# Last stage of an attention + expert + feed-forward kernel: slot outputs copied ahead of decoding, folding in three rounds, last 256 tokens with activations stationary, some low parts on VectorE, a new order

## The chip, the cores and the metric

The kernel runs on one core of a Trainium2 chip. The metric is the device time of one execution in microseconds; the kernel before has a median of 518.03 us over 3 runs (517.16 to 518.10). The profiled execution is one of its own.

## The reference, cut to what matters

```python
attn = softmax(mask(q @ k.T / 8)) @ v            # 4 batches, 12 heads, 448 tokens, 64 wide; causal
x = attn as (1792 tokens, 768)
logits = x @ phi                                  # 32 slots = 8 experts x 4
slot_input = softmax(logits over tokens).T @ x
slot_out = per expert: relu(slot_input @ w1[e]) @ w2[e]        # (32, 768)
y = softmax(logits over slots) @ slot_out          # (1792, 768)
h = y @ w_in                                       # w_in (768, 2048)
g = h * cos(h)
return g @ w_out                                   # w_out (2048, 768)
```

`w_in` and `w_out` come as float64 (two 32-bit words an element) and are turned into fp32 on the chip. All of it is computed at about fp32 precision.

## The kernel before, in words

The program has three stages. The first (to about 180 us) is the attention, with the slot logits and the slot inputs of each batch. The second (to about 236 us) streams 48 pieces of `w1` and `w2`, 1 MB each, through SBUF and ends with `slot_out`, transposed into `soT` (768 rows in six chunks of 128, 32 slots). It waits for the memory; `keep_warm` puts dummy matmuls between its pieces. The third, which the change is about, runs from there to the end.

The third stage never forms y. It folds `slot_out` into `w_in`: WS = slot_out @ w_in is only 32 x 2048, and h = softmax(logits) @ WS. WS and the softmax weights `CT` are kept in pieces of fp32r (a rounded fp32 that TensorE multiplies at full rate) stacked on 96 partitions, so that one matmul gives h at nearly fp32 precision. The hidden width 2048 is cut into 16 chunks `fc` of 128, the tokens into blocks of 512, 512, 512 and 256. A step is one chunk on one block, and `seq` (from SEQ, line 30) lists the 64 steps; the last 16 (s = 48 to 63) are the 256 tokens of block 3. The parts of a step, by their letters in the planner:

- H (`t_h`, L872): one matmul, h into one of two PSUM banks (6 and 7).
- Y, R, S, G (`t_y` L876 on ACT, `t_r` L879 on DVE, `t_s` L882 on ACT, `t_g` L885 on DVE): g = h cos(h) by range reduction and the sine table.
- K (`t_k`, L888, ACT): the high part of g in fp32r. L (`t_l`, L891, always POOL before): the low part, g minus its high part, from SBUF to SBUF.
- B (`back`, L898 to L900): for each of six 128-column groups m of `w_out`, three matmuls into bank m: high weights by high g, low weights by high g, high weights by low g. The weights are the stationary operand, the tokens are the moving one (512 columns, or 256 in block 3). The first step has its own order (`back0`, L908).
- F (`finish`, L915 to L921): bank m is added to or copied to SBUF at the end of a run of chunks, and after chunk 15 it goes out by a DMA on SP's queue. The output is held transposed, (768, 1792).

Each chunk needs two weight items of 768 KB: item 2c is `w_in`, item 2c+1 is `w_out`. Its decoding is a (`dec_a`, L706, ACT) and l, h, s (`dec_l`, `dec_h`, `dec_s`, L709, L713, L717, DVE, SBUF to SBUF). `w_out` is then split: u (`up_part`, L728, ACT) the high part in fp32r, v (`lo_part`, L741, DVE or POOL) the low part. `w_in` is folded for one or two chunks at a time (GRP, line 31): wm (`w_mm`, L839) multiplies six 128-row pieces by `soT`. A stationary `soT` chunk has 32 columns, so four such matmuls sit side by side, in four column groups of the array (r = ch % 4); w4 (L847, ACT) copies, wr (`w_rep`, L850, TensorE) adds the four groups, ws and wd (L854 ACT, L858 DVE) make WS.

A planner at the end of the file sets the order: it simulates the engines with a cost for each task (T, A, D, P for TensorE, ACT, DVE, POOL) and takes, whenever an engine is free, the ready task with the lowest key, its due time in steps. `port` keeps tasks of DVE and POOL apart that both work from SBUF to SBUF, with a tolerance (.35 before, L1034). The plan is written out as program order; each engine then works its list in order. `free` (L993) and the tasks `so` and `s,1` say when the second stage lets go of each engine.

Between the stages, in the last round of the second (L812 to L825, for piece 48), the order before is: `decode(1)`, i.e. item 1 on ACT and DVE; the copy of the last slot outputs `so` (L818, ACT); one `keep_warm`; two transposes (L823); the copy into `soT` (L824, DVE). `wm` of the first chunk needs that copy and item 0, which was decoded at piece 44.

## Time and profile before

| | |
|---|---|
| median of 3 runs | 518.03 us (517.16 to 518.10) |
| time of the profiled execution | 517.3 us |
| its span, first to last instruction | 515.5 us |
| TensorE (PE) busy | 488.3 us, 95% |
| VectorE (DVE), ScalarE (ACT), GpSimd (POOL) busy | 348.4, 313.5, 187.6 us |

Times in a profile are microseconds from the span's start unless marked ns. PE is TensorE's matmuls, PEld its weight loads, SP the engine that issues the DMAs. A matmul's end is modelled, so that two matmuls seem to overlap; the distance from one start to the next is what counts. L900 is line 900 of the kernel. In a timeline, the brackets give the idle time of the engine before the instruction and what ended it.

### The profile page before, as it was taken

Reading aid. Unit: us, or ns where it says so; the run is one execution under the profiler, and the core shown is the slowest. Engines: PE = TensorE matmul, PEld = TensorE weight load, DVE = VectorE, ACT = ScalarE, POOL = GpSimd, SP = SyncE. Lnnn points to the kernel's source line nnn. Section 1 sums busy time; section 2 is a strip of 40 time slices with the busy share of each in tenths; the row PEclk is TensorE's granted clock in tenths of the full one; section 3 lists DMA queues with packets and bytes.
Section 4 is the critical chain, followed back from the end, with each engine's and each line's share of the span. In section 5 each row is a group of like instructions: output and inputs, shape, how many; then the busy total and the mean of one; then the engine's idle time right before and its main releaser. Section 6 shows DMA issues by size and latency. Waiting matters only on the chain.

```text
span 515.5 us, 11275 instructions
## 1 busy us (share of the span) xinstructions
PE 488.3 (95%) x4308; PEld 357.3 (69%) x4308; DVE 348.4 (68%) x899; ACT 313.5 (61%) x745; POOL 187.6 (36%) x269
## 2 busy tenths in 40 slices
PE   8999999999999888877899999999999999999997
PEld 4766676776776342245667777888878778888996
DVE  4788888888884540025988899797989886355331
ACT  3999999989984201004867764747377555543552
POOL 1665556566540000001425252434442456322331
PEclk9999999999999999997999999999999999999999
DMA  5388788779757999999151533241353011113101
GB/s 198 99 292 296 279 291 292 282 269 337 266 209 261 402 422 419 420 419 359 65 184 61 191 118 123 67 173 65 123 191 116 1 62 73 51 67 116 63 1 62
DMA packets 24245, 100.37 MB, mean 195 GB/s; under 512 B 2816, under 2 KB 6912, under 8 KB 18048
## 3 DMA queue, kind: packets, MB, share of 16 engines
q1 hardware_dynamic: 24192, 99.66, 52.9%
q8 instruction: 34, 0.56, 0.4%
q14 instruction: 19, 0.16, 0.1%
HBM read 94.14 MB, written 5.51 MB: 193 GB/s over the span
## 4 chain that ended last, share of the span: by engine, by line
PE 59%; DVE 17%; ACT 10%; DMA 9%; POOL 2%; issue 2%; ACTq 0%; SPq 0%; POOLq 0%
PE bank L900 8%; PE bank L898 8%; PE bank L899 8%; PE bank L327 7%; PE bank L416 6%; DMA zraw<-in_w_out_dram 5%; PE bank L372 5%; PE bank L797 4%; DMA zraw<-in_w_in_dram 3%; PE bank L812 3%; DVE zscr L879 2%; DVE zscr L885 2%; POOL p L365 2%; ACT zraw L706 2%; ACT zscr L882 2%
## 5 line engine op out<-in xcount | busy, mean ns | idle before, releaser
L898 PE MATMUL bank<-zg,zhl 128*128 128x512 f32 (+1 forms) x378 | 139.7, 370 | 0.4 <-ACT zhl L728 0.4
L899 PE MATMUL bank<-zg,zhl 128*128 128x512 f32 (+1 forms) x378 | 137.5, 364 | 0.9 <-DVE zhl L741 0.9
L900 PE MATMUL bank<-zg,zhl 128*128 128x512 f32 (+1 forms) x378 | 137.2, 363 | 0.9 <-POOL zg L891 0.9
L891 POOL TENSOR_TENSOR zg<-zscr,zg 128x512 fp32r<-128x512 f32 (+1 forms) x64 | 82.7, 1298 | 139.2 <-ACT zg L888 125.4
L365 POOL TENSOR_SCALAR p<-p,pst 128x448 f32<-128x448 f32 (+3 forms) x161 | 79.0, 505 | 56.5 <-DVE pst L356 53.3
L345 ACT ACTIVATE p<-p,pst 128x448 f32<-128x448 f32 (+3 forms) x168 | 87.6, 523 | 13.2 <-DVE pst L343 11.3
L898 PEld LDWEIGHTS bank<-zg,zhl 128*128 128x128 f32 x378 | 71.4, 189 | 13.7 <-issue 1.2
L899 PEld LDWEIGHTS bank<-zg,zhl 128*128 128x128 f32 x378 | 71.5, 189 | 12.4 <-DVE zhl L741 1.4
L900 PEld LDWEIGHTS bank<-zg,zhl 128*128 128x128 f32 x378 | 71.4, 189 | 12.6 <-POOL zg L891 1.3
L882 ACT ACTIVATE zscr<-zscr,b_h 128x512 f32<-128x512 f32 (+1 forms) x64 | 42.0, 669 | 31.0 <-DVE zscr L879 30.8
L879 DVE SCALAR_TENSOR_TENSOR zscr<-zscr,bank 128x512 f32<-128x512 int32 (+1 forms) x64 | 38.8, 618 | 32.5 <-ACT zscr L876 32.2
L343 DVE CUSTOM_DVE_ANT_0 p<-bank,cs 128x448 f32<-128x448 f32 (+1 forms) x96 | 50.9, 548 | 6.4 <-PE bank L327 6.3
L327 PE MATMUL bank<-qk 64*128 64x320 f32 (+2 forms) x288 | 54.1, 472 | 0.0
L888 ACT ACTIVATE zg<-zscr 128x512 fp32r<-128x512 f32 (+1 forms) x64 | 36.3, 576 | 26.0 <-DVE zscr L885 25.8
L885 DVE TENSOR_TENSOR zscr<-bank,zscr 128x512 f32<-128x512 f32 (+1 forms) x64 | 39.2, 621 | 18.5 <-ACT zscr L882 18.4
L876 ACT ACTIVATE zscr<-bank,b_q 128x512 int32<-128x512 f32 (+1 forms) x64 | 39.4, 629 | 19.9 <-PE bank L872 19.8
L741 POOL TENSOR_TENSOR zhl<-uacc,zhl 128x768 fp32r<-128x768 f32 (+1 forms) x7 | 10.6, 1532 | 101.0 <-DMA zraw<-in_w_out_dram 85.9
L706 ACT ACTIVATE zraw<-zraw 128x768 f32<-128x768 f32 x32 | 29.2, 911 | 24.4 <-DMA zraw<-in_w_in_dram 13.1
L212 DVE COPY pts<-bank 128x512 f32<-128x512 f32 x48 | 32.8, 685 | 7.4 <-PE bank L372 6.9
L372 PE MATMUL bank<-cs,p 64*128 64x64 f32 (+1 forms) x768 | 35.3, 227 | 1.5 <-POOL p L365 1.4
L372 PEld LDWEIGHTS bank<-cs,p 64*128 64x128 f32 (+1 forms) x768 | 28.4, 133 | 11.1 <-POOL p L365 5.9
L345 ACT ACTIVATION_READ_ACCUMULATOR p<-p,pst 128x1 f32 x168 | 31.6, 188 | 0.0
(154 smaller groups left out, 695.3 us busy)
## 6 DMA issues: line engine op xcount, KB each, us to landing
w<-in_w_dram SPq DMA_DIRECT2D x48, 1024.0 KB, 8.5
zraw<-in_w_in_dram SPq DMA_DIRECT2D x16, 768.0 KB, 4.4
zraw<-in_w_out_dram SPq DMA_DIRECT2D x16, 768.0 KB, 4.3
qk<-in_qk_dram SPq DMA_DIRECT2D x24, 480.0 KB, 4.0
xk<-in_v_dram SPq DMA_DIRECT2D x12, 256.0 KB, 4.1
out_dram<-zps SPq DMA_DIRECT2D x8, 256.0 KB, 2.0
xts<-in_v_dram SPq DMA_DIRECT2D x12, 128.0 KB, 4.3
lt<-in_v_dram SPq DMA_DIRECT2D x12, 128.0 KB, 4.2
```

Of the source, the lines that this page charges most:

```text
L327: PE.matmul(sreg(j, c), lhsT=Q(p)[h, q0:q0 + 128], rhs=K(p)[h, 0:ln], start=True, stop=True)
L343: DVE.tensor_tensor_reduce(out=dst, in0=sb, in1=m, scale=-0.125, scalar=3.0e38, op0=ALU.add, op1=ALU.min, accum_out=st_[:, col:col + 1])
L345: return pr(f"exp{j}{c}")(lambda: ACT.activation(dst, dst, AF.Exp, bias=st_[:, col:col + 1], scale=-1.0, accum_out=st_[:, 8 + col:9 + col]))
L365: POOL.tensor_scalar(dst, dst, st_[:, 24 + col:25 + col], 0.0, op0=ALU.mult, op1=ALU.add)
L372: PE.transpose(out, src, by)
L879: DVE.scalar_tensor_tensor(y_(s), y_(s).bitcast(I32), -2.0 * math.pi, hb[:, 0:n_(s)], op0=ALU.mult, op1=ALU.add)
L882: ACT.activation(y_(s), y_(s), AF.Sin, bias=b_h, scale=1.0)
L885: DVE.tensor_tensor(y_(s), hb[:, 0:n_(s)], y_(s), ALU.mult)
L891: eng.tensor_tensor(g_(s)[1], y_(s), g_(s)[0].bitcast(F32), ALU.subtract)
L898: PE.matmul(o, lhsT=wh, rhs=gh, start=first, stop=False)
L899: PE.matmul(o, lhsT=wl, rhs=gh, start=False, stop=False)
L900: PE.matmul(o, lhsT=wh, rhs=gl, start=False, stop=last)
```

## The change

- **Between the stages.** `decode(1)` is taken apart: the copy `so` now comes first on ACT, then two `keep_warm` and `dec_a(1)`, the transposes, the copy into `soT` on DVE, two more `keep_warm`, and only then l, h, s of item 1 on DVE.
- **Folding.** For a pair of chunks, `w_mm` deals its twelve matmuls to the four column groups in three rounds of four, where they went in four rounds (four, two, four, two).
- **Last tokens.** In block 3, `back3` makes the 128 tokens of a half block the stationary operand and streams the weights: six triples of matmuls become four, of 512, 512, 256 and 256 columns, in three tasks (U3). `finish3` copies and sends the four banks in three DMAs of 256 KB, and these 256 tokens leave untransposed, so that the output tensor is one flat array with two parts. For chunks 12 to 15 the low parts are laid out so that each streamed segment is contiguous (`w_cols`).
- **Low parts.** L of the 17 steps in LE runs on DVE. Three v tasks have their engine set (VE).
- **Order.** The planner's costs, its start times, LA, the tolerance of `port` (.02) and many keys (KEYS) are new.

```diff
--- before.py
+++ after.py
@@ -30,9 +30,33 @@
 SEQ = ((0, 0, 2), (1, 0, 3), (2, 0, 4), (0, 2, 6), (1, 3, 8), (2, 4, 10), (0, 6, 13), (1, 8, 16), (2, 10, 16), (0, 13, 16), (3, 0, 16))
 GRP = ((0,), (1,), (2, 3), (4, 5), (6, 7), (8, 9), (10, 11), (12, 13), (14, 15))
 SAFE = 0.0
-LA = .4
+LA = 0.3
 KD = 0.0
 LD = False
+KEYS = {
+    ('B', 10, 0): 1, ('B', 10, 2): 1.5, ('B', 12, 2): 7, ('B', 12, 3): 8.75, ('B', 13, 0): 1, ('B', 13, 2): 7.25,
...
+    ('wr', 6): -6.75, ('wr', 8): -2.75, ('ws', 2): -3.5}
+VE = {11: 'P', 3: 'P', 6: 'D'}
+LE = {10: 'D', 11: 'D', 13: 'D', 15: 'D', 16: 'D', 2: 'D', 21: 'D', 26: 'D', 28: 'D', 30: 'D', 31: 'D', 32: 'D', 34: 'D', 43: 'D', 47: 'D', 7: 'D', 9: 'D'}
 KW = 3
@@ -667,7 +691,7 @@
         if c < 12:
             return [(ar[f"hl{c}"], 768 * u, 0, 6)]
         t = [ar[f"hl{3 * (c - 12) + i}"] for i in range(3)]
-        return [(t[0], 1536, 0, 4), (t[1], 1536, 4, 2)] if u == 0 else [(t[1], 1792, 0, 2), (t[2], 1536, 2, 4)]
+        return [(t[0], 1536, 0, 4), (t[1], 1536, 4, 2)] if u == 0 else [(t[2], 1536, 0, 4), (t[1], 1792, 4, 2)]
 
     def w_blk(c, u, m):
         for t, o, m0, nm in w_cols(c, u):
@@ -813,31 +837,41 @@
                                       start=(kc == 0), stop=(kc == 7))
                     if 42 <= npc[0] < 48:
                         keep_warm(3)
-                if npc[0] == 48:
-                    decode(1)
                 ACT.activation(so, sb[:, 0:256], AF.Copy)
                 tb = bank[6]
                 if npc[0] == 48:
-                    keep_warm(1)
+                    keep_warm(2)
+                    dec_a(1)
                 for c in range(2):
                     PE.transpose(tb[:, 128 * c:128 * c + 128], so[:, 128 * c:128 * c + 128], ident)
                 DVE.tensor_copy(soT[:, 2 * n:2 * n + 2, 16 * g:16 * g + 16].rearrange("p c (j t) -> p c j t", j=4),
                                 tb[:, 0:256].rearrange("p (c j t) -> p c j t", c=2, j=4)[:, :, :, 0:SPE])
+                if npc[0] == 48:
+                    keep_warm(2)
+                    dec_l(1)
+                    dec_h(1)
+                    dec_s(1)
 
     CT = ex["CT"]
     arena("WS", "scr", "g0", "g1", "ps", *[f"hl{i}" for i in range(12)], "ps2", "px")
     WS, scr = ar["WS"], ar["scr"]
+    oT = out[0:DM * TOK[3]].rearrange("(d t) -> d t", d=DM)
 
     def w4(q):
         n = len(GRP[q])
         return cs[:, 128 + 256 * (q % 2):128 + 256 * (q % 2) + 128 * n]
 
     def w_mm(q, wb):
-        for k_, n in enumerate(GRP[q]):
-            for ch in range(6):
-                r = ch % 4
-                PE.matmul(wb[32 * r:32 * r + 32, 128 * k_:128 * k_ + 128], lhsT=soT[:, ch, :],
-                          rhs=fwi(n)[:, 128 * ch:128 * ch + 128], start=(ch < 4), stop=(ch + 4 >= 6))
+
+        ts = [(0, 0, 0), (0, 1, 1), (0, 2, 2), (0, 3, 3), (0, 4, 0), (0, 5, 1)]
+        if len(GRP[q]) == 2:
+            ts += [(1, 0, 2), (1, 1, 3), (1, 2, 2), (1, 3, 3), (1, 4, 0), (1, 5, 1)]
+        seen = set()
+        for x, (k_, ch, r) in enumerate(ts):
+            PE.matmul(wb[32 * r:32 * r + 32, 128 * k_:128 * k_ + 128], lhsT=soT[:, ch, :],
+                      rhs=fwi(GRP[q][k_])[:, 128 * ch:128 * ch + 128], start=(k_, r) not in seen,
+                      stop=not any(y[0] == k_ and y[2] == r for y in ts[x + 1:]))
+            seen.add((k_, r))
 
     def wcols(q, wb):
         n = 128 * len(GRP[q])
@@ -907,6 +941,37 @@
             fc = seq[0][1]
             PE.matmul(bank[m][:, 0:n_(0)], lhsT=w_blk(fc, int(k_ == 1), m), rhs=gl if k_ == 2 else gh, start=k_ == 0,
                       stop=k_ == 2 and seq[0][3])
+
+    U3 = (((0, 0, 512, 0),), ((1, 0, 512, 2),), ((0, 512, 768, 1), (1, 512, 768, 3)))
+
+    def w_seg(fc, u, a, b):
+        for t, o, m0, nm in w_cols(fc, u):
+            if 128 * m0 <= a and b <= 128 * (m0 + nm):
+                return t[:, o + a - 128 * m0:o + b - 128 * m0]
+
+    def back3(s, k):
+
+        blk, fc, first, last = seq[s]
+        gh, gl = g_(s)
+        for k_, a, b, bn in U3[k]:
+            ob = bank[bn][:, 0:b - a]
+            th, tl = (g[:, 128 * k_:128 * k_ + 128] for g in (gh, gl))
+            wh, wl = w_seg(fc, 0, a, b), w_seg(fc, 1, a, b)
+            PE.matmul(ob, lhsT=th, rhs=wh, start=first, stop=False)
+            PE.matmul(ob, lhsT=th, rhs=wl, start=False, stop=False)
+            PE.matmul(ob, lhsT=tl, rhs=wh, start=False, stop=last)
+
+    def finish3(k, eng):
+        o3 = out[DM * TOK[3]:DM * NT].rearrange("(t p c) -> p t c", t=2, p=128)
+        if k < 2:
+            ob = ar["ps"][:, 512 * k:512 * k + 512]
+            copy("D" if eng is DVE else "A", ob, bank[(0, 2)[k]])
+            SP.dma_start(o3[:, k, 0:512], ob)
+            return
+        ob = ar["ps"][:, 1024:1536]
+        DVE.tensor_copy(ob[:, 0:256], bank[1][:, 0:256])
+        ACT.activation(ob[:, 256:512], bank[3][:, 0:256], AF.Copy)
+        SP.dma_start(o3[:, :, 512:768], ob.rearrange("p (t c) -> p t c", t=2))
 
     def finish(s, m, eng):
         blk, fc = seq[s][:2]
@@ -918,7 +983,7 @@
         else:
             ACT.activation(ob, o, AF.Copy)
         if fc == 15:
-            SP.dma_start(out[128 * m:128 * m + 128, TOK[blk]:TOK[blk + 1]], ob)
+            SP.dma_start(oT[128 * m:128 * m + 128, TOK[blk]:TOK[blk + 1]], ob)
 
 
 
@@ -931,10 +996,10 @@
     for j, (k_, c) in enumerate(items):
         key = need[GRP[qof[c]][0]] - 1.5 if k_ == "i" else need[c] - 0
         if j == 1:
-            task(("s", 1), dict(DMA=5.05), [], -2)
+            task(("s", 1), dict(DMA=5.2), [], -2)
         if j >= 2:
             if j >= NRAW:
-                task(("ld", j), dict(DMA=2.4), [("s", j - NRAW) if j > NRAW else None], j)
+                task(("ld", j), dict(DMA=3.9), [("s", j - NRAW) if j > NRAW else None], j)
             if k_ == "i":
                 fr = [("wm", qof[c - 4]) if c >= 4 else None]
             else:
@@ -949,16 +1014,20 @@
         if k_ == "o":
             task(("u", c), dict(A=.85), [("s", j)], key - 1.0)
             task(("v", c), dict(P=1.9, D=.9), [("u", c)], key - .6, True)
-    task(("so",), dict(DMA=5.199999999999999), [], -1)
+    task(("so",), dict(DMA=2.75), [], -1)
     for q, grp in enumerate(GRP):
         key = need[grp[0]] - 1.5
         n = len(grp)
-        task(("wm", q), dict(T=.3 + .45 * n), [("s", 2 * c) for c in grp if c] + [("w4", q - 2) if q >= 2 else None, ("so",)], key - .8)
+        task(("wm", q), dict(T=.14 + .22 * (n + 1)), [("s", 2 * c) for c in grp if c] + [("w4", q - 2) if q >= 2 else None, ("so",)], key - .8)
         task(("w4", q), dict(A=.15 + .11 * n), [("wm", q)] + [("wr", q - 2) if q >= 2 else None], key - .7)
-        task(("wr", q), dict(T=.3 + .22 * n), [("w4", q)], key - .6)
+        task(("wr", q), dict(T=.1 + .22 * n), [("w4", q)], key - .6)
         task(("ws", q), dict(A=.15 + .11 * n), [("wr", q)], key - .5)
         task(("wd", q), dict(D=.17 + .13 * n), [("ws", q)], key - .4)
     pb = {}
+
+    def nu(s):
+        return 3 if seq[s][0] == 3 else 6
+
     for s, (blk, fc, first, last) in enumerate(seq):
         w = n_(s) / 512.0
         task(("H", s), dict(T=.02 + .22 * w), [("wd", qof[fc]), ("H", s - 1) if s else None], s - 3)
@@ -966,31 +1035,41 @@
         task(("R", s), dict(D=.07 + .54 * w), [("Y", s)], s - 2.5)
         task(("S", s), dict(A=.1 + .56 * w), [("R", s)], s - 2.4)
         task(("G", s), dict(D=.07 + .54 * w), [("S", s)], s - 2.3)
-        task(("K", s), dict(A=.1 + .46 * w), [("G", s), ("B", s - 4, 5) if s >= 4 else None], s - 1.7)
-        task(("L", s), dict(P=.07 + 1.2 * w, D=.07 + .55 * w) if LD else dict(P=.07 + 1.2 * w), [("K", s)], s - 1.5, True)
+        task(("K", s), dict(A=.1 + .46 * w), [("G", s), ("B", s - 4, nu(s - 4) - 1) if s >= 4 else None], s - 1.7)
+        task(("L", s), dict(D=.07 + .55 * w) if LE.get(s) == "D" else dict(P=.07 + 1.3 * w), [("K", s)], s - 1.5, True)
         if s == 0:
             task(("B", 0, 0), dict(T=1.4), [("K", 0), ("u", 0)], .0)
             task(("B", 0, 1), dict(T=1.4), [("B", 0, 0), ("v", 0)], .1)
             task(("B", 0, 5), dict(T=1.4), [("B", 0, 1), ("L", 0)], .2)
-        for m in range(6):
+        for m in range(nu(s)):
             if s == 0:
                 if last:
                     task(("F", s, m), dict(D=.61) if m % 2 == 0 else dict(A=.5), [("B", 0, 5)], s + .2 + m / 10)
                     pb[m] = ("F", s, m)
                 continue
-            pv_ = ("B", s, m - 1) if m else (("B", s - 1, 5) if s else None)
+            pv_ = ("B", s, m - 1) if m else (("B", s - 1, nu(s - 1) - 1) if s else None)
+            if blk == 3:
+                task(("B", s, m), dict(T=(.68, .68, .73)[m]), [("K", s), ("L", s), ("u", fc), ("v", fc), pv_, *([pb.get(x) for x in ((0,), (2,), (1, 3))[m]] if first else [])], s + m / 10)
+                if last:
+                    task(("F", s, m), (dict(D=.61), dict(A=.5), dict(D=.35))[m], [("B", s, m)], s + .2 + m / 10)
+                continue
             task(("B", s, m), dict(T=.01 + .67 * w), [("K", s), ("L", s), ("u", fc), ("v", fc), pv_, pb.get(m) if first else None], s + m / 10)
             if last:
                 seen = any(t[0] == blk and t[3] for t in seq[:s])
                 task(("F", s, m), dict(D=.07 + .54 * w) if seen or m % 2 == 0 else dict(A=.08 + .42 * w), [("B", s, m)], s + .2 + m / 10)
                 pb[m] = ("F", s, m)
+    for t, x in KEYS.items():
+        T[t] = T[t][:2] + (T[t][2] + x,) + T[t][3:]
+    for c, e in VE.items():
+        T["v", c] = ({e: T["v", c][0][e]},) + T["v", c][1:]
     LAT = dict(T=.24, A=.17, D=.1, P=.1, DMA=.9)
     succ, nd, tr_ = {}, {}, {}
     for t, (e, d, _, _) in T.items():
         nd[t], tr_[t] = len(d), 0.0
         for x in d:
             succ.setdefault(x, []).append(t)
-    free = dict(T=6.0, A=5.6, D=5.95, P=3.0)
+    free = dict(T=3.6, A=3.95, D=6.05, P=3.0)
+    free0 = dict(free)
     TIMED = {("so",): 0, ("s", 1): 0, ("raw", 2): 0, ("raw", 3): 0}
     for t, x in ((("raw", 2), 4.9), (("raw", 3), 6.8)):
         T[t] = (dict(DMA=x - .9),) + T[t][1:]
@@ -1031,7 +1110,7 @@
                 eng, _, key, pt = T[t]
                 if e not in eng:
                     continue
-                if pt and e in port and port["P" if e == "D" else "D"] > now + .35:
+                if pt and e in port and port["P" if e == "D" else "D"] > now + .02:
                     continue
                 if t[0] in ("H", "wm") and min(hbf) > now + 1e-9:
                     continue
@@ -1056,7 +1135,7 @@
                 fin = eng[e]
             elif e == "DMA":
                 st_ = max(now, free[e])
-                fin = free[e] = st_ + eng[e]
+                free[e], fin = st_ + 1.9, st_ + eng[e]
             else:
                 fin = free[e] = st_ + eng[e]
             if pt and e in port:
@@ -1080,7 +1159,7 @@
             now = min(nxt)
 
     bk = lambda t: bank[6 + hbo[t]]
-    run = dict(ld=ld, a=dec_a, l=dec_l, h=dec_h, s=dec_s, u=up_part, S=t_s, K=t_k, B=lambda s, m: (back if s else back0)(s, m))
+    run = dict(ld=ld, a=dec_a, l=dec_l, h=dec_h, s=dec_s, u=up_part, S=t_s, K=t_k, B=lambda s, m: (back3 if seq[s][0] == 3 else back if s else back0)(s, m))
     run.update(H=lambda s: t_h(s, bk(("H", s))), Y=lambda s: t_y(s, bk(("H", s))), R=lambda s: t_r(s, bk(("H", s))),
                G=lambda s: t_g(s, bk(("H", s))))
     for nm, fn in (("wm", w_mm), ("w4", w_4), ("wr", w_rep), ("ws", w_s), ("wd", w_d)):
@@ -1097,7 +1176,7 @@
             elif t[0] == "L":
                 t_l(t[1], ENG[e])
             elif t[0] == "F":
-                finish(t[1], t[2], ENG[e])
+                finish3(t[2], ENG[e]) if seq[t[1]][0] == 3 else finish(t[1], t[2], ENG[e])
             else:
                 run[t[0]](*t[1:])
 
...
```

## Rows read from the trace of the kernel before

**Rows 1.** The page, part 1: busy time of each engine.
```profile
PE 488.3 (95%) x4308; PEld 357.3 (69%) x4308; DVE 348.4 (68%) x899; ACT 313.5 (61%) x745; POOL 187.6 (36%) x269
```

**Rows 2.** Stretches of 20 us: busy time (instructions) by engine, granted clock, DMA share.
```profile
240.00:260.00 20.00, 18.39 (x94) 14.52 (x93) 17.13 (x25) 15.48 (x26) 8.07 (x5) 0.91 0.35 123
...
300.00:320.00 20.00, 19.23 (x103) 15.26 (x103) 19.09 (x25) 11.78 (x19) 7.84 (x5) 1.00 0.32 102
```

**Rows 3.** Who PE waited for, from 246.9 us on: total, times, longest.
```profile
PE bank L872 <- DVE zscr L885: 1.6, 3, 0.8
PE bank L872 <- DVE zWS L858: 1.5, 2, 0.8
PE bank L899 <- DVE zhl L741: 0.9, 1, 0.9
PE bank L900 <- POOL zg L891: 0.9, 1, 0.9
```

**Rows 4.** Timeline between the second and the third stage: start, duration, engine, line.
```profile
233.73 1.05 PE L812 MATMUL bank<-w,dk 128*4 128x256 f32 x16 [0.58 <-DMA w<-in_w_dram]
...
235.65 0.90 ACT L706 ACTIVATE zraw<-zraw 128x768 f32<-128x768 f32 x1 [9.52 <-DMA zraw<-in_w_out_dram]
236.44 0.37 ACT L818 ACTIVATE cs<-bank 128x256 f32<-128x256 f32 x1
...
238.45 0.18 DVE L824 COPY dT<-bank 128x32 f32<-128x32 f32 x1
...
238.69 1.07 PE L839 MATMUL bank<-zfa,dT 128*32 128x128 f32 x12 [1.13 <-DVE dT L824]
...
246.93 4.26 PE L908 MATMUL bank<-zg,zhl 128*128 128x512 f32 x18
```

**Rows 5.** Timeline of the same hand-over one round earlier.
```profile
223.78 1.05 PE L812 MATMUL bank<-w,dk 128*4 128x256 f32 x16 [0.57 <-DMA w<-in_w_dram]
...
224.96 0.39 ACT L818 ACTIVATE cs<-bank 128x256 f32<-128x256 f32 x1 [8.13 <-PE bank L812]
...
225.95 0.19 DVE L824 COPY dT<-bank 128x32 f32<-128x32 f32 x1 [8.41 <-PE bank L823]
```

**Rows 6.** Timeline of one folded pair and the matmul behind it.
```profile
260.26 1.07 PE L839 MATMUL bank<-zfb,dT 128*32 128x128 f32 x24
...
261.26 0.50 PE L898 MATMUL bank<-zg,zhl 128*128 128x512 f32 x1
```

**Rows 7.** Timeline at the change from 512-token to 256-token steps.
```profile
474.17 0.39 PE L898 MATMUL bank<-zg,zhl 128*128 128x512 f32 x1
...
475.30 0.39 PE L900 MATMUL bank<-zg,zhl 128*128 128x512 f32 x1
...
475.88 0.28 PE L872 MATMUL bank<-CT,zWS 96*128 96x256 f32 x1
...
478.16 0.28 PE L872 MATMUL bank<-CT,zWS 96*128 96x256 f32 x1
```

**Rows 8.** Timeline at a low part of weights on POOL beside decoding on DVE.
```profile
296.11 1.84 POOL L741 TENSOR_TENSOR zhl<-lt,zhl 128x768 fp32r<-128x768 f32 x1 [6.12 <-ACT zhl L728]
296.26 2.50 DVE L713 SCALAR_TENSOR_TENSOR zfb<-zraw,zfb 128x768 int32<-128x768 int32 x1
```

**Rows 9.** Groups by line and shape, from 200 us on: busy us, mean ns.
```profile
L891 POOL TENSOR_TENSOR zg<-zscr,zg 128x512 fp32r<-128x512 f32 x48 | 70.9, 1483 | 110.9 <-ACT zg L888 98.7 <-issue 5.9 <-PE bank L899 2.5
...
L741 DVE TENSOR_TENSOR zhl<-lt,zhl 128x768 fp32r<-128x768 f32 x4 | 4.3, 1069 | 2.3 <-ACT zhl L728 2.3
```

**Rows 10.** Timeline of the end: last matmul, last output DMA.
```profile
511.52 0.28 PE L900 MATMUL bank<-zg,zhl 128*128 128x256 f32 x1
...
512.88 0.40 SPq L921 DMA_DIRECT2D out_dram<-ctok  x1
```

**Rows 11.** DMA issues: count, KB each, median us from issue to landing.
```profile
out_dram<-zps SPq DMA_DIRECT2D x8, 256.0 KB, 2.0
...
out_dram<-zps SPq DMA_DIRECT2D x4, 128.0 KB, 1.8
```

More of the change, by code (lines that the diff above doesn't have):

```diff
@@ L1156 @@
         args.append(nc.dram_tensor(f"in_{name}_dram", a.shape, mybir.dt.from_np(a.dtype), kind="ExternalInput").ap())
-    args.append(nc.dram_tensor("out_0_dram", (DM, NT), F32, kind="ExternalOutput").ap())
+    args.append(nc.dram_tensor("out_0_dram", (DM * NT,), F32, kind="ExternalOutput").ap())
     with tile.TileContext(nc) as tc:
@@ L1162 @@
     order = [1, 3, 4, 5, 6, 2, 0]
+    n = NT - 256
+    got = np.concatenate([got[:DM * n].reshape(DM, n), got[DM * n:].reshape(256, DM).T], axis=1)
     got = got.reshape(DM, NB, 7, 64)[:, :, [order.index(i) for i in range(7)]].reshape(DM, NT)
```

19 rows, old and new, of the table KEYS are left out of this document.

## The prediction

> **What bounds the kernel now.** I read the page's part 1 first: TensorE (PE) is busy for 95% of the span, and no other engine over 68% [rows 1]. That is an average, so the stretches of the third stage came next, where the whole change lies. In 300 to 320 us PE is busy 19.23 of 20 us, but DVE 19.09 as well; in 240 to 260 us, the stage's start, PE has 18.39, DVE 17.13, and the granted clock's mean is 0.91, which between full and half level is 3.6 us at 1.2 GHz [rows 2]. So PE is the bound, with DVE close behind it. What PE waits for tells where DVE comes through: from the first B on, these waits sum to 4.9 us, 3.1 of them H (L872) behind DVE, 0.9 the low weights of the second chunk made by DVE, 0.9 a low part L made by POOL [rows 3]. Every matmul pass saved in the third stage should come off the end; every microsecond saved elsewhere counts only if it brings PE's first B forward or fills one of these waits.
>
> **The start of the stage.** The last w2 matmuls start at 233.73. ACT then takes the decoding of item 1 first (235.65 for 0.90, when its DMA lands) and the slot copy after it, at 236.44; DVE copies into `soT` at 238.45, after all of item 1's decoding, and the folding begins at 238.69 [rows 4]. One round earlier, with nothing in front, the slot copy starts 1.18 us after the w2 matmuls' start and the DVE copy 0.99 after that [rows 5]. With the slot copies ahead of decoding: 233.73 + 1.18 + 0.99 + 0.24 (copy to folding, as in rows 4) = 236.14, against 238.69: 2.5 us. The added `keep_warm` behind the transposes may hold PE for a tenth or two, so 2.4. The price is small: item 1's l step waits for the `soT` copy until about 236.1, but h waits for `dec_a` until 236.55 anyway, so decoding ends where it ended.
>
> From folding to the first B the chain takes 246.93 - 238.69 = 8.24 us [rows 4], through ACT and DVE in turn, and moves as a whole. What is late next is the second chunk: already now its low weights make PE wait 0.9 us [rows 3], and DVE has only 2.9 us idle in that window [rows 2]. I therefore take 2.2 of the 2.4. The ends: 0, if the second chunk's decoding holds the next B where it is; and 2.4 + 1.2 = 3.6, if besides PE, with more to do, is not put to 1.2 GHz, where the first folding took 1.07 us [rows 4], as long as a pair with twice the matmuls at full level [rows 6]; three such short PE steps in the chain give an estimated 3 x 0.4.
>
> **Folding.** A pair takes 261.26 - 260.26 = 1.00 us of PE [rows 6] in four rounds, so a round is at most 0.25; something of it is fixed, so I take 0.2 for the round that goes. GRP has seven pairs: 1.5 us (0 if the groups wait for each other, 1.75 at most). It is PE time in the middle of the stage, where PE is the bound.
>
> **Last tokens.** A step of block 3 now takes 478.16 - 475.88 = 2.28 us from H to H: 19 matmuls of 256 columns at 0.120. Five 512-column matmuls take 475.30 - 474.17 = 1.13, so 0.226 each, not 0.240 [rows 7]: 0.0135 us of each matmul doesn't depend on its width. The new step has H, six of 512 and six of 256: 0.12 + 6 x 0.226 + 6 x 0.12 = 2.20. Sixteen steps of 0.08 are 1.3 us, all PE's own. The columns streamed stay the same; what goes is six fixed parts a step. The ends are 0 and 16 x 0.1.
>
> The rows show 13.5 ns beyond the width [rows 7]. The Trainium skill (TensorE: Matmul & The Clock Gate, "Wait — 56ns, not 53.3ns?") puts the fixed cost of a warm matmul at about 2.5 ns. By that figure, an estimate, six fewer a step would give 0.24 us in all and the sum would end 1.1 us later; the kernel's own pitches decide for me.
>
> **The end.** The last DMA is issued 1.36 us after the last matmul's start (512.88 - 511.52), behind five others on SP's queue [rows 10]; it lands 1.8 us later, a 256 KB one 2.0 [rows 11]. With three DMAs, the last behind two copies that run side by side, I take the issue 0.4 earlier and the landing 0.2 later: 0.2 us (0.6 lost to 0.6 won, if the three big transfers queue or SP's queue had been all of the delay).
>
> **Low parts on DVE, and the order.** L takes POOL 1.48 us on average; the nearest row for DVE is the 768-column low part at 1.07, or 0.71 for 512 columns [rows 9]. So 17 steps give POOL 25 us back and cost DVE 12.1. PE waits for POOL only 0.9 us in all, so POOL's time is worth little by itself. But POOL's work stretches DVE's: a decoding step begun 0.15 us after a POOL low part took 2.50 us and ended 0.81 after it [rows 8]; PE's H soon afterwards is one of those that wait for DVE. The new order plans nearly no overlap of the two (.02 for .35), so such stretches should become rarer. The rows can't show how a new order falls out. Of the 4.0 us of waits that are left after the start's 0.9 [rows 3], I take 1.0 back. The ends: 4.0 won, and 7.0 lost if much of the 12.1 meets PE's path.
>
> **The sum.** Against the profiled execution's 517.3 us (span 515.5 and 1.8 around it): 2.2 + 1.5 + 1.3 + 0.2 + 1.0 = 6.2, so 511.1. The median of the runs, 518.03, is 0.7 above that execution; on its scale I say 511.4.
>
> **Rivals.**
> - *The start gains nothing.* The second chunk's decoding on DVE, not the fold chain, decides when B runs on; the 2.2 turn into a longer wait, and the order gives nothing. For it: 0.9 us of just this wait and DVE's 17.13 of 20 [rows 2, 3]. Against it: DVE still has 2.9 us idle there, mostly behind the chain. 517.3 - 1.5 - 1.3 - 0.2 = 514.3.
> - *The waits vanish too.* Clock kept, DVE never late: 517.3 - 3.6 - 1.5 - 1.3 - 0.2 - 4.0 = 506.7. For it: the waits are few and long (the longest 0.8 to 0.9 us [rows 3]), so each is a place in the order rather than a lack of throughput. Against it: DVE at 19.09 of 20 [rows 2].
> - *DVE becomes the bound, and the kernel slower.* Place: the middle of the stage, where DVE has 0.9 us idle in 20 [rows 2] and L's of 0.71 come on top. Price: up to the 12.1. Without the waits' 1.0 the forecast is 512.1; slower by 0.2% needs 7.0 of the 12.1, ten L's of 17, on PE's path; with twelve it is 512.1 + 8.5 = 520.6. Against it: fewer stretches such as the one of rows 8, and PE's 3.1 us of waits for DVE in the whole stage.
> - *The change doesn't do what it says on PE.* The three rounds run as four, and streaming the weights at 512 doesn't pitch at 0.226 when the stationary operand changes with every other one: 517.3 - 2.2 - 0.2 - 1.0 = 513.9.
>
> **How the numbers follow.** The forecast has 0.45 (its own range 509 to 513.5), no gain at the start 0.18, no waits 0.22, no PE saving 0.08, DVE the bound 0.07. The range from 506.5 to 515.2 takes in the first four with the bounds of their small terms. About 0.2%, 1.0 us, is what a measurement tells from no change. Slower has 0.05 (the DVE rival past ten L's), within 0.2% another 0.05 (that rival short of it, and no gain at the start with lost waits), faster 0.90.
>
> **What would show it.** Slot copy at about 235.0 and folding at about 236.2; the first B near 244.5; a pair 0.8 us from its first matmul to the next one; steps of 2.20 us in block 3, with twelve matmuls behind H; the last DMA about 1 us after the last matmul; PE's waits from the first B on near 3 us. I am wrong if the second chunk's B still starts near 252, if the DVE waits of H grow past 5 us, or if PE's matmuls of the last 16 steps take no less than 2.28 us a step.

## The result, and the profile after

The changed kernel has a median of 512.75 us (512.27 to 513.61, 4 runs) against 517.83. The ratio on record is 0.9913, with a 95% interval of 0.9896 to 0.9929 (these two medians alone would give 0.9902). That is 5.1 us by the medians and 4.5 by the ratio, where my sum had 6.2; the direction and both ranges hold. The path there isn't the one that I described.

The page's part 1, and two stretches of 20 us (busy time of PE, PEld, DVE, ACT, POOL with instructions, granted clock, DMA share, GB/s):

```profile
PE 486.5 (95%) x4240; PEld 354.7 (69%) x4240; DVE 348.8 (68%) x911; ACT 311.7 (61%) x744; POOL 164.9 (32%) x252
```

```profile
240.00:260.00 20.00, 14.16 (x72) 10.47 (x71) 17.72 (x23) 12.72 (x20) 6.48 (x4) 0.84 0.41 136
300.00:320.00 20.00, 20.00 (x109) 15.96 (x108) 18.73 (x28) 14.26 (x23) 5.27 (x3) 1.00 0.46 158
```

The shares answer to [rows 1] and hardly moved. The stretches answer to [rows 2] and did, in opposite directions: the start of the stage got worse (PE 14.16 us busy for 18.39, at a lower mean clock), its middle got full (20.00 for 19.23). Whom PE waited for, from 244 us to the end, answers to [rows 3]:

```profile
PE bank L906 <- DVE zscr L919: 4.0, 1, 4.0
PE bank L942 <- ACT zg L922: 1.7, 1, 1.7
PE bank L934 <- POOL zg L925: 0.2, 1, 0.2
```

There are three waits, all before 260 us. Behind them, none is left. The 1.7 us lie ahead of the first B; from there on PE waits 4.2 us, where it waited 4.9 before. The timeline of the start shows how they come about (start, duration, engine, line; compare [rows 4]):

```profile
233.85 1.05 PE L836 MATMUL bank<-w,dk 128*4 128x256 f32 x16 [0.57 <-DMA w<-in_w_dram]
...
235.03 0.38 ACT L840 ACTIVATE cs<-bank 128x256 f32<-128x256 f32 x1 [8.77 <-PE bank L836]
...
235.94 0.19 DVE L847 COPY dT<-bank 128x32 f32<-128x32 f32 x1 [7.02 <-PE bank L846]
...
236.28 0.63 PE L871 MATMUL bank<-zfa,dT 128*32 128x128 f32 x12
...
240.66 1.83 POOL L765 TENSOR_TENSOR zhl<-uacc,zhl 128x768 fp32r<-128x768 f32 x1 [84.02 <-ACT zhl L752]
240.97 2.33 DVE L737 SCALAR_TENSOR_TENSOR zfa<-zraw,zfa 128x768 int32<-128x768 int32 x1
...
243.83 0.94 DVE L741 SCALAR_TENSOR_TENSOR zfa<-zraw,zfa 128x768 int32<-128x768 int32 x1
...
244.62 1.66 PE L942 MATMUL bank<-zg,zhl 128*128 128x512 f32 x6 [1.71 <-ACT zg L922]
244.64 1.30 POOL L925 TENSOR_TENSOR zg<-zscr,zg 128x512 fp32r<-128x512 f32 x1 [2.15 <-ACT zg L922]
244.69 2.07 DVE L737 SCALAR_TENSOR_TENSOR lt<-zraw,lt 128x768 int32<-128x768 int32 x1
...
248.98 0.29 DVE L892 TENSOR_TENSOR zWS<-bank,zWS 32x128 fp32r<-32x128 f32 x1 [0.68 <-ACT zWS L888]
...
249.87 0.63 PE L906 MATMUL bank<-CT,zWS 96*128 96x512 f32 x2
...
254.47 0.79 PE L906 MATMUL bank<-CT,zWS 96*128 96x512 f32 x1 [3.98 <-DVE zscr L919]
...
255.14 0.79 PE L932 MATMUL bank<-zg,zhl 128*128 128x512 f32 x1
...
259.24 0.63 PE L934 MATMUL bank<-zg,zhl 128*128 128x512 f32 x1
...
259.67 0.63 PE L932 MATMUL bank<-zg,zhl 128*128 128x512 f32 x1
```

Slot copy, fold and first B come where I put them (235.03, 236.28, 244.62). Then the second chunk is late. Two of its decoding steps on DVE take 2.33 and 2.07 us, each begun beside POOL's work, and the second step's B starts at 255.14; before it was 251.78. Three lines of the kernel before go with this:

```profile
240.20 0.96 DVE L717 SCALAR_TENSOR_TENSOR zfa<-zraw,zfa 128x768 int32<-128x768 int32 x1
...
246.35 0.74 PE L872 MATMUL bank<-CT,zWS 96*128 96x512 f32 x2 [0.30 <-DVE zWS L858]
...
251.78 0.50 PE L898 MATMUL bank<-zg,zhl 128*128 128x512 f32 x1 [0.37 <-ACT zhl L728]
```

The delay lies ahead of the second and third H, which start together at 249.87 and started at 246.35: from there to the second step's B it takes 5.3 us, before 5.4. The first of these two H's needs the folding of chunk 1, and that needs item 2, whose decoding ends at 244.77 (243.83 + 0.94) and ended at 241.16. Of these 3.6 us, 1.4 are the stretch of the 2.33 us step. The rest is the order: the steps of item 2 now stand further back in DVE's list. The 2.07 us step, of item 3, doesn't hold the two H's: behind it DVE still waits 0.68 us for ACT before it finishes the WS for them.

From the trace's matmul starts I worked out where each step's first B stands against the kernel before (us, negative is earlier; step 0 is the first step):

```
step   0     1     2     4     6     12    20    36    40    48    63    last matmul
      -2.3  +3.4  +6.1  +3.3  +2.3  +0.2  -0.6  -2.4  -3.2  -3.0  -4.1  -4.1
```

From step 1 to step 2 it takes 8.27 us, before 5.57. Most of that goes with the clock. PE had waited since 250.5 when the granted clock fell to 1.2 GHz at 253.77; it stayed there to 260.59, and 512-column matmuls started 0.43 us apart (259.24 to 259.67) instead of 0.23. I estimate 2.7 us for it, half of the time from 255.14 to 260.59. The kernel before had 6.8 us at 1.2 GHz too, but from 236.61 to 243.44, ahead of its first B. Another 0.8 of the +6.1 is order alone (the folding of chunks 2 and 3 now stands ahead of step 2's B) and comes back later; against these, a wait of 0.9 us in the old second step is gone. From step 2 to block 3 the changed kernel gains 9 us, in block 3 another 1.2.

One folded pair and the matmul behind it, for [rows 6]: 0.79 us from start to start, where it was 1.00.

```profile
289.41 0.86 PE L871 MATMUL bank<-zfa,dT 128*32 128x128 f32 x24
290.20 0.50 PE L932 MATMUL bank<-zg,zhl 128*128 128x512 f32 x1
```

In block 3, for [rows 7], three streams of 512 columns take 0.70 us (475.60 to 476.30), not 0.68:

```profile
475.60 0.39 PE L960 MATMUL bank<-zhl,zg 128*128 128x512 f32 x1
475.83 0.40 PE L961 MATMUL bank<-zhl,zg 128*128 128x512 f32 x1
476.07 0.39 PE L962 MATMUL bank<-zhl,zg 128*128 128x512 f32 x1
476.30 0.28 PE L960 MATMUL bank<-zhl,zg 128*128 128x256 f32 x1
```

And the end, for [rows 10]: the last DMA is issued 0.73 us after the last matmul, earlier than I thought, yet the span ends 4.2 us after it (511.6 - 507.38), before 4.0.

```profile
507.38 0.28 PE L962 MATMUL bank<-zhl,zg 128*128 128x256 f32 x1
...
508.11 0.39 SPq L974 DMA_DIRECT2D out_dram<-zps  x1
```

### The profile page after: what moved, and what is told of

It reads as the page before. It is cut to its first block, busy times and chain, and to the rows that moved or that the text cites. A ratio compares the mean times of both kernels' runs of the same rounds, so it can differ in the third digit from the quotient of the medians.

```text
span 511.6 us, 11140 instructions
## 1 busy us (share of the span) xinstructions
PE 486.5 (95%) x4240; PEld 354.7 (69%) x4240; DVE 348.8 (68%) x911; ACT 311.7 (61%) x744; POOL 164.9 (32%) x252
## 4 chain that ended last, share of the span: by engine, by line
PE 73%; DMA 14%; DVE 5%; ACT 3%; POOL 3%; issue 1%; POOLq 0%; ACTq 0%; SPq 0%
DMA w<-in_w_dram 12%; PE bank L932 12%; PE bank L934 12%; PE bank L933 12%; PE bank L351 7%; PE bank L440 7%; PE bank L396 5%; PE bank L906 2%; PE bank L960 2%; PE bank L961 2%; PE bank L962 2%; POOL p L389 2%; PE bank L557 1%; PE bank L544 1%; DMA zraw<-in_w_out_dram 1%
## 5 line engine op out<-in xcount | busy, mean ns | idle before, releaser
L932 PE MATMUL bank<-zg,zhl 128*128 128x512 f32 x282 | 113.5, 403 | 0.0
L934 PE MATMUL bank<-zg,zhl 128*128 128x512 f32 x282 | 111.0, 394 | 0.2 <-POOL zg L925 0.2
L933 PE MATMUL bank<-zg,zhl 128*128 128x512 f32 x282 | 111.0, 394 | 0.0
L925 POOL TENSOR_TENSOR zg<-zscr,zg 128x512 fp32r<-128x512 f32 (+1 forms) x47 | 55.2, 1176 | 137.0 <-ACT zg L922 99.4
L932 PEld LDWEIGHTS bank<-zg,zhl 128*128 128x128 f32 x282 | 53.6, 190 | 13.2 <-issue 1.4
L934 PEld LDWEIGHTS bank<-zg,zhl 128*128 128x128 f32 x282 | 53.5, 190 | 12.4 <-POOL zg L925 0.9
L933 PEld LDWEIGHTS bank<-zg,zhl 128*128 128x128 f32 x282 | 53.6, 190 | 11.1
L765 POOL TENSOR_TENSOR zhl<-uacc,zhl 128x768 fp32r<-128x768 f32 (+2 forms) x9 | 14.0, 1570 | 109.7 <-ACT zhl L752 109.7
```

The costliest lines, as they stand in the source:

```text
L925: eng.tensor_tensor(g_(s)[1], y_(s), g_(s)[0].bitcast(F32), ALU.subtract)
L932: PE.matmul(o, lhsT=wh, rhs=gh, start=first, stop=False)
L933: PE.matmul(o, lhsT=wl, rhs=gh, start=False, stop=False)
L934: PE.matmul(o, lhsT=wh, rhs=gl, start=False, stop=last)
```

## The experiments

The medians of before stood at 517.52 to 517.58 us beside these runs, and each ratio is against those runs. The changed kernel was not run again beside them: where I say slower or faster than it, I compare a median with its 512.75.

**In the old order: each part alone.** Hand-over, folding, last tokens and low parts were each put into the kernel before.

```diff
 # b_head: the last round of the second stage
-                if npc[0] == 48:
-                    decode(1)
                 ACT.activation(so, sb[:, 0:256], AF.Copy)
...
+                    keep_warm(2)
+                    dec_a(1)
```

> The kernel before with the hand-over alone changed (slot outputs copied ahead of decoding); its order and everything else stay. Theory 1 (the prediction's): folding starts 2.4 us earlier, the chain moves as a whole and 2.2 us come off the end: about 515.6 where before has 517.8. Theory 2 (the second chunk's decoding on DVE holds the second B): the first B comes 2.3 us earlier, the second stays where it is (its low weights ready at about 253 us), and the end moves by 0 to 0.5 us.

Measured: 518.40, ratio 1.0028 (1.0011 to 1.0045), slower by a little. The timeline of its hand-over:

```profile
235.54 0.63 PE L843 MATMUL bank<-zfa,dT 128*32 128x128 f32 x12
...
236.87 0.91 ACT L706 ACTIVATE zraw<-zraw 128x768 f32<-128x768 f32 x1 [0.89 <-DMA zraw<-in_w_in_dram]
...
237.68 0.26 ACT L851 ACTIVATE cs<-bank 128x128 f32<-128x128 f32 x1
...
239.53 0.96 DVE L717 SCALAR_TENSOR_TENSOR zfa<-zraw,zfa 128x768 int32<-128x768 int32 x1
...
240.52 0.29 DVE L862 TENSOR_TENSOR zWS<-bank,zWS 32x128 fp32r<-32x128 f32 x1
...
240.86 0.79 PE L876 MATMUL bank<-CT,zWS 96*128 96x512 f32 x1 [1.75 <-DVE zWS L862]
...
247.32 4.28 PE L912 MATMUL bank<-zg,zhl 128*128 128x512 f32 x18
```

Folding starts 3.15 us earlier than in [rows 4] (0.6 of it because the second stage ended that much earlier in this execution), but the engines work their lists in order. ACT has a decoding step ahead of the chain's copy, which waits for its DMA until 236.87; DVE has the whole of item 2 ahead of the chain's `wd`. The first B is at 247.32, not even earlier. Neither theory had that: the chain doesn't move as a whole, because its links are nailed to places in the lists. PE was also granted only 1.2 GHz from 240.33 to 247.15, where before had it from 236.61 to 243.44; how much of the late B is the clock's, no run tells.

```diff
 # b_fold: w_mm
-        for k_, n in enumerate(GRP[q]):
-            for ch in range(6):
-                r = ch % 4
-        ...
+        ts = [(0, 0, 0), (0, 1, 1), (0, 2, 2), (0, 3, 3), (0, 4, 0), (0, 5, 1)]
+        ...
```

> The kernel before with the three rounds of folding alone. Theory 1 (PE is the bound): a pair takes 0.80 us instead of 1.00 to the next matmul, seven pairs give 1.4 to 1.5 us. Theory 2 (DVE or ACT is the bound where the pairs stand): the pairs get shorter, but PE's waits for DVE grow by as much, and the end moves by under 0.5 us.

Measured: 517.30, ratio 1.0012 (0.9988 to 1.0035), no change. Its seven pairs do take 0.79 us each. But PE's waits from 246.4 us on are 7.3 us, where [rows 3] sum to 4.9; these are the largest:

```profile
PE bank L877 <- DVE zscr L890: 2.3, 4, 0.9
PE bank L877 <- DVE zWS L863: 2.1, 2, 1.1
PE bank L904 <- DVE zhl L741: 0.9, 1, 0.9
PE bank L855 <- ACT cs L852: 0.9, 3, 0.4
```

So theory 2: in the old order PE's 1.5 us turned into waits for DVE and ACT.

```diff
 # b_last: U3, back3, finish3 and their tasks; the flat output
...
-    run = dict(... B=lambda s, m: (back if s else back0)(s, m))
+    run = dict(... B=lambda s, m: (back3 if seq[s][0] == 3 else back if s else back0)(s, m))
```

> The kernel before with the last 256 tokens alone changed (activations stationary, three output DMAs of 256 KB). Theory 1: steps of 2.20 us instead of 2.28, 1.2 to 1.3 us by the last matmul; the end behind it is 0.2 us longer (as in the changed kernel, 4.2 against 4.0 us), so 1.0 to 1.1 us in all. Theory 2 (the pitch is not PE's own): nothing.

Measured: 515.93, ratio 0.9977 (0.9956 to 0.9999). About 1.2 us by the ratio, near theory 1, but with a wide interval: six of its runs took 514.01 to 515.26 and six 516.60 to 517.91. In its profile the 15 steps from s = 48 to 63 take 0.7 us less than before, and 4.2 us follow the last matmul's start for 4.0, so the part itself is worth 0.5 to 0.6 there, less than theory 1 says.

That profile also stands 1.9 us ahead of before at s = 48, though DVE and POOL work the same lists in both up to about 395 us. In [rows 8] DVE began 0.15 us after POOL; here it began 0.01 us ahead of it, and POOL was the one to be stretched:

```profile
295.90 0.96 DVE L713 SCALAR_TENSOR_TENSOR zfb<-zraw,zfb 128x768 int32<-128x768 int32 x1
295.91 2.67 POOL L741 TENSOR_TENSOR zhl<-lt,zhl 128x768 fp32r<-128x768 f32 x1 [6.18 <-ACT zhl L728]
```

Behind it DVE stands 1.2 us further ahead, and 2.0 after a second such place at 311 us. So one execution can differ from the next by as much as a part is worth.

```diff
 # b_ldve
-                t_l(t[1], ENG[e])
+                t_l(t[1], DVE if t[1] in LE else POOL)
```

> The kernel before with the low parts of the same 17 steps on DVE, each in the same place of the program; nothing else. Theory 1 (a low part on DVE takes collisions away in any order): PE's waits fall from 5 us to 3, 515.5. Theory 2 (it pays only where the order leaves DVE room for it, as with folding and the hand-over, which gave nothing in the old order): 0 to 3 us slower than before, 517.6 to 520.6, in waits of H and of the low parts for DVE.

Measured: 518.25, ratio 1.0017 (0.9995 to 1.0039): nothing gained, as theory 2 says at its lower end. The waits for DVE fell a little, and a new one came, for an ACT copy of the fold chain (2.6 us in two waits).

**In the new order: each part undone.** The plan is kept; only the part goes back.

```diff
 # a_fold4: w_mm as before        # a_nohead: decode(1) first again
 # a_lpool
-                t_l(t[1], ENG[e])
+                t_l(t[1], POOL)
```

> The changed kernel with the old folding in four rounds; its order stays. Theory 1 (in the new order PE is the bound where the pairs stand, since its waits are gone; in the old order the saved time went into waits for DVE): 1.2 to 1.5 us slower than the changed kernel, about 514.1. Theory 2 (the pairs' time is hidden in the new order as well): no difference, 512.7.

Measured: 514.29, ratio 0.9943 (0.9921 to 0.9965): 1.5 us slower than the changed kernel, by medians. The intervals still overlap, but the seven pairs take 1.00 us again, which is 7 x 0.21 = 1.5 us of PE. Theory 1.

> The changed kernel with the old hand-over (item 1 decoded ahead of the slot copies); its order stays. Theory 1 (the second step's B hangs on DVE's list, which begins with the first chunk's chain, so that the chain's start moves the list): folding 2.4 us later, the first B at about 247, the second at about 257, 1.5 to 2.4 us slower than the changed kernel, 514.3 to 515.2. Theory 2 (the second chunk's decoding is the limit by itself): the second B at 255, no difference.

Measured: 515.19, ratio 0.9968 (0.9951 to 0.9984): 2.4 us slower, theory 1. The fold starts at 238.76, and the first 20 steps all stand 1.8 to 2.0 us later; the fourth H still waits 3.98 us:

```profile
256.50 0.80 PE L902 MATMUL bank<-CT,zWS 96*128 96x512 f32 x1 [3.98 <-DVE zscr L915]
```

> The changed kernel with the 17 low parts of LE put back on POOL, each in the same place of the program; the order stays. Theory 1 (low parts on DVE took collisions of POOL and DVE away, and so PE's waits): decoding steps of 2 us and more come back, PE waits 3 to 5 us more, about 516. Theory 2 (the order alone did it): within 0.7 us of 512.75. Theory 3 (DVE paid for them): 1 to 2 us faster.

Measured: 514.92, ratio 0.9949 (0.9930 to 0.9968): 2.2 us slower, between theories 1 and 2 but on the side of 1. The decoding steps h and s that DVE ran between 256 and 460 us, in groups by line and tile (busy us, mean ns), first with these low parts on POOL, then in the changed kernel:

```profile
L737 DVE SCALAR_TENSOR_TENSOR zfb<-zraw,zfb 128x768 int32<-128x768 int32 x7 | 9.2, 1316 | 0.0
L737 DVE SCALAR_TENSOR_TENSOR zfa<-zraw,zfa 128x768 int32<-128x768 int32 x6 | 7.8, 1300 | 0.1
...
L741 DVE SCALAR_TENSOR_TENSOR zfa<-zraw,zfa 128x768 int32<-128x768 int32 x6 | 7.8, 1305 | 0.0
```

```profile
L737 DVE SCALAR_TENSOR_TENSOR zfb<-zraw,zfb 128x768 int32<-128x768 int32 x7 | 6.9, 980 | 0.0
...
L737 DVE SCALAR_TENSOR_TENSOR zfa<-zraw,zfa 128x768 int32<-128x768 int32 x6 | 5.7, 951 | 0.1
L741 DVE SCALAR_TENSOR_TENSOR zfa<-zraw,zfa 128x768 int32<-128x768 int32 x6 | 5.6, 948 | 0.0
```

Summed over all eight groups of that answer, these steps take 61.6 us with the low parts on POOL and 52.7 without. The l steps of the same answer take 19.7 and 17.0. So moving the low parts gives DVE 11.6 us back, and the 16 of them in this window cost it 11.6 (all 17 cost 12.2, 17 x 0.721, from the groups of the changed kernel). DVE is not relieved; it is made punctual, and PE's waits behind 256 us fall from 1.9 us to 0.2.

```diff
 # a_oldlast
-        return 3 if seq[s][0] == 3 else 6
+        return 6
...
 # a_orderonly: that, and the three parts above undone as well
```

> The changed kernel with the old last 256 tokens (weights stationary, six output DMAs); the order up to step 48 is the same. Theory 1 (all of it is PE's pitch, as predicted): 1.3 us by the steps and 0.2 at the end, 514.2. Theory 2 (a matmul that changes its width costs some ns more, so a step gives 0.063 and not 0.084 us, and the three big DMAs take 0.2 us longer at the end): 0.7 to 0.8 us, 513.5.

Measured: 513.72, ratio 0.9931 (0.9910 to 0.9952). By medians 1.0 us for the last tokens, between the theories and nearer 2; the interval can't tell them apart. The traces are with theory 2: in the same order block 3 gives 0.9 us up to the last matmul, and the end takes 0.2 of it back.

> The changed kernel with all four parts undone (old hand-over, four rounds, old last tokens, low parts of LE on POOL) and only its order kept. Theory 1 (the parts add up in the new order): 512.75 + 2.4 (hand-over) + 1.5 (folding) + 2.2 (low parts) + 0.8 (last tokens) = 519.7, slower than before. Theory 2 (the order is worth most of the gain by itself, and the parts overlap): 514 to 516.

Measured: 520.92, ratio 1.0057 (1.0036 to 1.0078): slower than before by 3.0 us in the ratio, theory 1. This order was planned for the four parts, and alone it loses; the parts then bring 2.4 + 1.5 + 2.2 + 1.0 = 7.1 us, from 520.9 to 513.8, within about 1 us of what was measured. In its profile PE is granted 1.2 GHz for 6.8 us twice in the third stage, from 237.66 and from 258.14, where before has one such stretch; how much of the 3.0 us that is, no run tells.

**The clock in the wait.** Between 253.77 and 260.59 us the changed kernel's PE was granted 1.2 GHz, in the last 0.7 us of its wait of 4.0 and behind it. I filled the wait with matmuls that add zeros.

```diff
+        zz = ar["hl0"][:, 1536:1664].bitcast(F32)
+        POOL.memset(zz, 0.0)
...
+            if t == ('H', 2):
+                for _ in range(32):          # 16 in the second run
+                    PE.matmul(bank[3][:, 0:128], lhsT=zz, rhs=ident, start=False, stop=False)
```

> The changed kernel with 32 matmuls by a zero stationary operand added, between the two H's behind the first B and the third H, where PE waits 4.0 us and then runs 6.8 us at 1.2 GHz. They add zeros to a bank, so nothing else changes but a 64 KB memset on POOL. Theory 1 (the fall of the clock there is on the path): no stretch at 1.2 GHz at the second and third step, the third step's B starts at about 260 instead of 263.4, and 2.5 to 3.4 us come off the end. Theory 2 (DVE holds the steps behind anyway): the third step is earlier, but PE's waits for DVE come back in the next 60 us and the end moves by less than 1 us.

Measured: 516.30, ratio 0.9982 (0.9967 to 0.9996). I had taken a matmul's time for its half: the 32 took 7.1 us and delayed the second step's B to 257.66. The run still says something. It shows no time at 1.2 GHz between 180 and 510 us, and at full level PE waited for DVE in the folding ahead of the third step. The second step took 6.54 us instead of 8.27, yet at the fifth step the run stood 2.6 us behind the changed kernel again:

```profile
261.17 0.63 PE L871 MATMUL bank<-zfb,dT 128*32 128x128 f32 x12
262.59 0.63 PE L871 MATMUL bank<-zfb,dT 128*32 128x128 f32 x12 [0.79 <-DVE zfb L741]
```

> The changed kernel with 16 matmuls by a zero stationary operand in PE's 4.0 us wait behind the first B. In the run with 32 they took 7.1 us (each is two instructions of 0.11), so that they delayed the second step by 2.5 us themselves; 16 take 3.6 and fit. Theory 1 (the clock's fall there is on the path): the second step's B at 255.1 as before, the third at about 260.5 instead of 263.4, and the end 2.5 to 3.4 us earlier, 509.4 to 510.3 against 512.75. Theory 2 (DVE holds the steps behind): under 1 us, with PE's waits for DVE back between 260 and 320 us.

Measured: 513.34, ratio 0.9924 (0.9900 to 0.9948), no gain. In its profile a stretch at 1.2 GHz came anyway, for 3.4 us from 257.7, and the third step's B started where it does in the changed kernel. Over its six runs the mean clock was 0.996 to 0.997 in three (513.22 to 513.46) and 0.992 in three (512.65 to 514.12), so the time doesn't follow the mean clock. But that mean is over the whole span, and the profiled run was at 1.2 GHz for 3.4 us near 169 us as well: it doesn't tell in which stretch the runs differ. The two runs lean to theory 2; that the clock costs nothing there isn't shown, as no run of mine had full level and an undelayed second step.

**Another choice of keys.**

```diff
-    ('B', 10, 0): 1, ('B', 10, 2): 1.5, ...
+    ...                                   # other keys; 14 steps in LE, 12 chunks in VE
```

> The changed kernel with other keys and other steps in LE and VE (14 low parts of g on DVE, the first chunk's low weights on DVE, not POOL), chosen so that the second step's B comes earlier. Theory 1 (POOL's work stretches DVE's decoding ahead of the second step): the two decoding steps of 2.1 to 2.3 us there are 1 us again, the second step's B starts 0.5 to 1 us earlier and the end moves by 0.5 to 1.5 us, to 511.5. Theory 2: what the start gains, waits behind it take back, 512.7.

Measured: 513.17, ratio 0.9902 (0.9873 to 0.9931): the same as the changed kernel (one of its six runs took 509.60, the others 512.11 to 513.98). The second step's B starts at 255.17, as there; the first, 1.4 us earlier, only lengthens the wait for DVE (4.6 us at its longest). The two decoding steps that were stretched there take 0.95 us each here. But another is now stretched beside POOL, right ahead of the second step's R:

```profile
243.24 1.66 PE L1806 MATMUL bank<-zg,zhl 128*128 128x512 f32 x6 [0.32 <-ACT zg L1786]
...
249.63 1.80 POOL L1629 TENSOR_TENSOR zhl<-lt,zhl 128x768 fp32r<-128x768 f32 x1 [93.70 <-ACT zhl L1616]
...
249.75 2.50 DVE L1601 SCALAR_TENSOR_TENSOR zfb<-zraw,zfb 128x768 int32<-128x768 int32 x1
...
252.28 1.28 DVE L1777 SCALAR_TENSOR_TENSOR zscr<-zscr,bank 128x512 f32<-128x512 int32 x2
```

So theory 1 wasn't tested cleanly: every run in the new order has such a stretch at the start of the stage.

## Why the prediction was right, and where it was wrong

**Start.** Sized right by the wrong mechanism, which is luck. I took 2.2 us and undoing the hand-over costs 2.4. But "the chain moves as a whole" failed: in the old order its links stayed where the lists held them, and the first B came at 247.32. Only the new order turns the earlier fold into an earlier list of DVE. My check ("wrong if the second chunk's B still starts near 252") came out against me: 255.14. What was late next I had named, the second chunk, but priced at 0.2. I had let item 1's decoding end where it ended; it ends at 239.39 for 238.53, because its last step now stands behind the chain's wd in DVE's list. Item 2 is then 3.6 us late, 1.4 of it by a stretched step, and PE waits 4.0. The condition of my upper end did come: PE kept full level to 253.77 and the first folding took 0.63 us for 1.07. But from folding to the first B it took 8.34 us, before 8.24, because the stretched step stands ahead of the first step's G in DVE's list; in a_search, without that stretch, it took 6.96 (236.28 to 243.24). The stretch at 1.2 GHz came later, on the second step's matmuls. The rival in which the start gains nothing describes the first 20 us better than my forecast.

**Folding.** 0.21 a pair, 1.5 us, as said (my own 7 x 0.2 would have been 1.4), and a pair of 0.8 us as said. The condition "where PE is the bound" did all the work: it holds in the new order and failed in the old one.

**Last tokens.** Direction right, size too big: I had 1.3 us and 0.2 at the end. Four steps from s = 48 take 8.87 us (472.57 to 481.44), before 9.11: 0.06 a step, not 0.084, so 1.0 in all; undoing the part in the same order gives 0.9. The mis-sized term is the pitch of a 512-column matmul, 0.226 by [rows 7]: in block 3 the three take 0.70. The rows didn't show a stream that changes between two widths. At the end the issue came 0.63 us earlier than before, where I took 0.4, but what follows it, to the end of the span, took 3.5 us for 2.6: 0.2 lost for 0.2 won. Both ends were in my bounds. By the Trainium skill's fixed cost of about 2.5 ns a matmul (TensorE: Matmul & The Clock Gate, "Wait — 56ns, not 53.3ns?") the 96 matmuls that went would be worth an estimated 0.24 us; the steps, at 1.0, go with the kernel's own pitches.

**Low parts and order.** I took 1.0 of the 4.0 us of waits back. Behind 260 us all of them went, as in my rival with no waits, and the start gave most of it away again: from the first B on PE waits 4.2 us, where I had said near 3. That the two errors nearly cancel is why the sum was near, and that is luck. By the runs with parts undone, order and low parts together lose 0.8 us (3.0 lost, 2.2 won back) where I had 1.0 won. The reason that I gave, POOL's work stretching DVE's, holds: 11.6 us of stretch went with the low parts. The price of 12.1 us on DVE was right too (12.2), and it didn't meet PE's path; the slower rival failed on that. What I didn't see is that the order by itself is 3 us slower than the old one, and that the parts don't pay without it: I priced five terms one by one, and three of them are worth nothing alone.

**The sum.** My 6.2 us off the runs' 518.03 make 511.8; the 511.4 that I said took 0.4 more than the sum had.

## What to carry to other kernels

Where engines work fixed lists, an earlier result pays only if the lists behind it are ordered for it: price a part together with the order it runs in, and test it by undoing it in the new order as well as by doing it in the old. An engine near full load can be helped by taking its long stalls away even where its work stays the same. Where PE's waits are few and long, follow the instruction that ended each back through its chain; here one wait of 4.0 us led back to decoding that stood late in DVE's list, with one step of it stretched to more than twice its time.

## What the runs showed of the hardware that I had not expected

Three 512-column matmuls with alternating stationary halves, next to 256-column ones, take 0.70 us instead of 0.68; what costs the 7 ns each is open. A DVE step begun 0.31 us into a POOL low part of 1.83 us took 2.33 us, and ended 0.81 us after it (240.97 to 243.30, against 242.49). An undisturbed one takes 0.95, so it moved little until POOL was done. The Trainium skill (SBUF — State Buffer, "Who interferes with whom") has it that a DVE instruction with two SBUF inputs contends with a POOL instruction that reads SBUF, and calls the ports that they share an exclusive lock; this trace agrees. Which of the two is stretched went by which began first: begun 0.15 us behind POOL, a DVE step took 2.50 us and POOL 1.84 [rows 8]; begun 0.01 us ahead, in b_last, the same step took 0.96 and POOL 2.67.
